# Load order, raw buffers, early counts and late gates in the second mixture of an attention and two-mixture kernel

## Chip, cores and metric

One core of a Trainium2 chip runs the whole program. The metric is device time in microseconds (us), the median of three runs.

## The reference

```
def _attn_ref(q, k, v):                 # 2 x 8 heads x 576 positions x 64
    scores = q @ k.T / 8, masked to the last 64 positions; softmax; @ v
def _moe_ref(x, domain_probs, w1, w2):  # 1152 rows x 512, 4 experts, F = 1024
    p = domain_probs / sum;  out = sum over e of p[:, e] * (relu(x @ w1[e]) @ w2[e])
def _moe2_ref(x, w_skip, w_gate, w1, w2):   # 8 experts
    do_compute = (x @ w_skip) > 0
    e_idx = argmax(x @ w_gate);  gate_w = softmax(x @ w_gate)[e_idx]
    out = x;  out[row] += gate_w * (relu(x[row] @ w1[e_idx]) @ w2[e_idx])   # where do_compute
```

In the first mixture every expert works on every row. In the second each row goes to one expert at most, so the kernel sorts rows by expert and works on blocks of 128 of them. With these inputs the eight experts get 116, 207, 129, 66, 298, 17, 114 and 51 rows.

## The kernel before, in words

The inputs are f32. Each operand is split into a high part of type f32r and a low part (the rest), and a product is three matmuls: high by high, high by low, low by high. ScalarE (ACT) writes the high part as a copy, VectorE (DVE) the low part as a subtraction. So a weight goes through a load by SP into a `raw` tile of 512 KB (`w_load`, L310), a copy by ACT (`hi`, L331, 1024 columns) and a subtraction by DVE (`lo`, L335); only then is the raw tile free. An expert has four chunks of first weights (L315 in the trace) and four of second weights (L317). Two sets of weight tiles, `wa` and `wb`, serve the experts in turn, and `w_pass` (L987) adds the loads and splits of one expert's first or second weights.

There are two rings of raw tiles: `raw`, four tiles in memory that is there from the start, and `raw2` (`M["raw"]`), four tiles in memory that `open_moe2` (L829) opens. `extra` in `w_pass` picks the ring. `open_moe2` closes the pool `h` (the 18 KB a partition of `x2`, and 12 KB each of `hh` and `hl`) and the pool `rt` with tiles of the routing, and opens in their place, from the right, `mg` (18 KB), `mo` (20 KB) and `mr` (16 KB, `raw2`). A tile in a pool that lies where a closed pool was waits for all instructions on the closed pool's tiles, also for those that the program lists later.

The order of work on every engine is written by a planner (`Plan`, L92). `add` hands it an operation with an engine, an assumed duration, what it reads and writes, a priority and a slack that is added to its ready time. `run` places the operations one by one, each time the one that can start first (priority breaks ties), and then emits them sorted by planned start. An engine executes its own operations in just that order. On ACT and DVE an operation of priority 0 or more may not run over the ready time of one of negative priority by more than 0.2 (L162). Loads count 1.46 on SP and 1.1 latency, apart from early ones (`early`, the first weights of expert 3 and later), which are put on an engine "X" that costs nothing else. Operations on X, such as `open_moe2` and `counts`, only fix a place in the program.

The first plan covers attention, the first mixture, the routing and block 0 of expert 0 of the second mixture. Each later expert has one plan for its first block (`block`, L881) and, if it has more rows, further ones under a branch: `tails` (L1084) asks whether it has more than 128. A block takes 20 matmuls of its first product, then transposes (`tr`, L927): ACT copies the product out (`hr`, L921), PE transposes it (L938), ACT and DVE write the high and low part of `ht` (L942, L945); this is done in two pieces. 24 matmuls of the second product follow, and DVE multiplies by the gates and adds (L979). Rows are fetched by indirect DMAs of GpSimd (POOL; `gather`, L845) and written by others (`scatter`, L854). During an expert's block its plan also holds the loads and splits of the next expert's weights and the transposes of the next rows (`xpose`, L861).

The routing (`route`, L625) runs once for each of nine row tiles t: logits, best expert, rank, and a product `tab` (L742) that puts row numbers (its columns 0 and 1) and gates (columns 2 to 4, the gate in three bf16 parts) into a table. For the last two tiles the gate columns are done late: `gate` (L723), `spread` with its `wx` (L737), `tab`. `idx` (L791) makes the row numbers, `num` (L803) the counts, `rest` (L812) the gates and the scatter's row numbers. `counts` (L1048) loads the packed counts into a register of every engine (L1050), and `hint` (L1077) tells PE's instruction fetch which way a later branch will go. After the last expert comes a deep section (L1121) under a branch of its own, for experts with more than 384 rows; here it is jumped over.

## Time and profile before

| | |
|---|---|
| median of three runs | 675.88 us (675.45 to 675.97) |
| the profiled execution | 672.51 us |
| its span, first to last instruction | 670.8 us |
| granted TensorE clock, mean | 0.984 |
| PE busy | 628.2 us, 94% |
| second mixture | from 486.9 us to the end |

Times in the rows are us from the span's start. PE is TensorE's matmuls, PEld its weight loads, SPq the queue of SP. A bracket at the end of a row gives how long the engine stood idle before it and what released it. [...]

### The profile page before, as it was taken

The numbers are of one execution on the slowest core, as the hardware profiler recorded it, in microseconds if no ns is written. First come the engines' busy times: TensorE is split into PE (matmuls) and PEld (weight loads), VectorE is DVE, ScalarE is ACT, GpSimd is POOL, SyncE is SP. The second block draws the span as 40 slices with busy tenths as digits, with TensorE's granted clock in tenths as the row PEclk, the third lists the DMA queues.
The fourth block names the chain that finished last, engine by engine and source line by source line (L and its number), as shares of the span: only waits on it lengthen the run. The fifth ranks groups of instructions, "written<-read, shape, count | busy, mean of one in ns | idle before, by whom it ended". The sixth has DMA issues, their size and how long they took to land. (4 is left out here: it accounts for less than half of the span.)

```text
span 670.8 us, 9656 instructions
## 1 busy us (share of the span) xinstructions
PE 628.2 (94%) x3652; PEld 552.8 (82%) x3652; DVE 323.8 (48%) x699; ACT 237.0 (35%) x492; POOL 91.5 (14%) x112
## 2 busy tenths in 40 slices
PE   6889999999999999999999999999987899899783
PEld 6788899898989898989898989898965678687573
DVE  5997932137312136212136336265576575654661
ACT  4974741035202033202033202124326465634550
POOL 6541320000000000000000000000043142312510
PEclk9999999999999999999999999999989999899987
DMA  9668000008300005200004210113339957961631
GB/s 219 159 164 241 23 4 1 0 1 270 106 1 1 0 1 176 75 1 1 0 1 165 87 64 33 48 47 104 129 131 308 360 185 227 303 252 39 209 112 29
DMA packets 55851, 71.69 MB, mean 107 GB/s; under 512 B 32953, under 2 KB 32953, under 8 KB 55776
## 3 DMA queue, kind: packets, MB, share of 16 engines
q1 hardware_dynamic: 52912, 62.17, 29.1%
q0 software_dynamic: 2864, 8.54, 4.4%
q8 instruction: 44, 0.72, 0.4%
q14 instruction: 31, 0.25, 0.1%
HBM read 64.00 MB, written 7.47 MB: 107 GB/s over the span
## 5 line engine op out<-in xcount | busy, mean ns | idle before, releaser
L523 PE MATMUL mm<-xth,wa1h 128*128 128x384 f32 (+1 forms) x416 | 137.4, 330 | 0.0
L523 PE MATMUL mm<-xtl,wa1h 128*128 128x384 f32 (+1 forms) x416 | 135.3, 325 | 0.0
L523 PE MATMUL mm<-xth,wa1l 128*128 128x384 f32 (+1 forms) x416 | 135.2, 325 | 0.0
L529 ACT ACTIVATE hh<-mm 128x384 fp32r<-128x384 f32 (+1 forms) x104 | 48.5, 466 | 234.5 <-PE mm L523 225.9
L544 PE MATMUL mm<-wa2h,hh 128*128 128x512 f32 (+1 forms) x296 | 116.9, 395 | 0.0
L544 PE MATMUL mm<-wa2h,hl 128*128 128x512 f32 (+1 forms) x296 | 115.0, 389 | 0.0
L544 PE MATMUL mm<-wa2l,hh 128*128 128x512 f32 (+1 forms) x296 | 114.9, 388 | 0.0
L531 DVE SCALAR_TENSOR_TENSOR hl<-mm,hh 128x384 fp32r<-128x384 f32 (+1 forms) x104 | 54.5, 526 | 121.7 <-ACT hh L529 121.6
L523 PEld LDWEIGHTS mm<-xth,wa1h 128*128 128x128 f32 x416 | 78.3, 188 | 0.7
L523 PEld LDWEIGHTS mm<-xtl,wa1h 128*128 128x128 f32 x416 | 78.2, 188 | 0.5
L523 PEld LDWEIGHTS mm<-xth,wa1l 128*128 128x128 f32 x416 | 78.2, 188 | 0.0
L544 PEld LDWEIGHTS mm<-wa2h,hl 128*128 128x128 f32 x296 | 55.7, 188 | 12.4
L544 PEld LDWEIGHTS mm<-wa2l,hh 128*128 128x128 f32 x296 | 55.8, 189 | 11.1
L544 PEld LDWEIGHTS mm<-wa2h,hh 128*128 128x128 f32 x296 | 55.8, 188 | 11.0
L556 DVE SCALAR_TENSOR_TENSOR x<-mm,prob,x 128x512 f32<-128x512 f32 (+1 forms) x28 | 20.5, 732 | 91.2 <-PE mm L544 91.2
L766 POOL DMA_INDIRECT x<-scr,id x1 | 1.2, 1242 | 360.3 <-DVE id L783 360.3
L331 ACT CAST wa2h<-raw 128x1024 fp32r<-128x1024 f32 x32 | 33.3, 1053 | 28.0 <-PE mm L544 18.6
L335 DVE TENSOR_TENSOR wa1l<-raw,wa1h 128x1024 fp32r<-128x1024 f32 x31 | 36.9, 1220 | 9.6 <-ACT wa1h L331 9.0
L335 DVE TENSOR_TENSOR wa2l<-raw,wa2h 128x1024 fp32r<-128x1024 f32 x30 | 36.2, 1219 | 7.0 <-ACT wa2h L331 6.8
L331 ACT CAST wa1h<-raw 128x1024 fp32r<-128x1024 f32 x30 | 30.3, 1047 | 22.5 <-DMA raw<-in_moe_w_dram 16.0
L855 POOL DMA_INDIRECT out_dram<-xg,ids x11 | 16.1, 1460 | 86.9 <-DVE xg L979 59.5
L444 POOL TENSOR_TENSOR s<-s,mx 128x512 f32<-128x512 f32 x18 | 20.2, 1122 | 50.1 <-DVE mx L441 23.0
(203 smaller groups left out, 917.8 us busy)
## 6 DMA issues: line engine op xcount, KB each, us to landing
raw<-in_moe_w_dram SPq DMA_DIRECT2D x96, 512.0 KB, 5.5
scr<-x SPq DMA_DIRECT2D x9, 256.0 KB, 2.1
out_dram<-x SPq DMA_DIRECT2D x9, 256.0 KB, 2.3
qn<-in_q_dram SPq DMA_DIRECT2D x8, 256.0 KB, 4.0
kn<-in_k_dram SPq DMA_DIRECT2D x8, 256.0 KB, 4.1
vn<-in_v_dram SPq DMA_DIRECT2D x8, 256.0 KB, 4.7
qn<-in_q_dram SPq DMA_DIRECT2D x2, 128.0 KB, 4.4
kn<-in_k_dram SPq DMA_DIRECT2D x2, 128.0 KB, 4.4
```

What stands on the lines that cost most here:

```text
L331: (POOL.tensor_copy if hpool else DVE.tensor_copy if hdve else ACT.copy)(out=aps()[0], in_=b.tile)
L335: (POOL if pool else DVE).tensor_tensor(out=l, in0=b.tile, in1=f32(h), op=ALU.subtract)
L444: add("POOL", 1.0, lambda: POOL.tensor_tensor(out=s.tile, in0=s.tile, in1=mx[:, 3].unsqueeze(2).to_broadcast([128, HP, 128]), op=ALU.mult) ...
L523: PE.matmul(out=ps[:, 0:n], lhsT=wa[a][:, kk, f * 128:(f + 1) * 128], rhs=x[:, kk, g0:g0 + n], start=(i == 0), stop=(i == 3 * KC - 1))
L529: add("ACT", c_act(n), lambda: ACT.activation(out=hh[:, f, 0:n], in_=ps[:, 0:n], func=ACTF.Relu), rd=[ps], wr=[("hh", f)], prio=-1)
L531: add("DVE", c_dve(n), lambda: DVE.scalar_tensor_tensor(out=hl[:, f, 0:n], in0=ps[:, 0:n], scalar=0.0, in1=f32(hh[:, f, 0:n]), op0=ALU.max ...
L544: PE.matmul(out=ps[:, 0:c1 - c0], lhsT=x[:, f, o:o + 128], rhs=wa[a][:, f, c0:c1], start=(f == 0 and i == 0), stop=(f == FC - 1 and i == 2))
L556: DVE.scalar_tensor_tensor(out=z, in0=y, scalar=prob[:, t, e:e + 1], in1=z, op0=ALU.mult, op1=ALU.add)
L766: add("POOL", 1.0, lambda: POOL.indirect_dma_start(out=R["x0"], out_offset=None, in_=scr[0:128 * (GT + 1), :], in_offset=bass.IndirectOffs ...
L855: add("POOL", 1.0, lambda: POOL.indirect_dma_start(out=out, out_offset=bass.IndirectOffsetOnAxis(ap=R["ids"][0:n, j, e:e + 1], axis=0), in ...
```

## The change

- Load order: an early load costs 0.0 instead of 0.01 in the planner.
- Raw buffers: second weights of every expert from 1 on go to `raw2` (before: from 2 on, by a counter).
- Gates: those of the last two tiles, and `rest`, are added inside block 0 of expert 0, and read the low part of the second piece of `ht` (`htl`, 4). The tiles they use move from the pool `rt` to `rc`, with a `wy` of their own beside `wx`. Masks move to an attention pool.
- Counts and hint: `counts` no longer waits for the second product of expert 0, and `hint` for expert 0 follows the second group of its first product. `num` writes a third value, loaded as `nv[2]`: the last expert has more than 128 rows, or one has more than 384.
- The transposes beside expert 0's second product come after its group 3.
- The last two transposes and logits of the routing get a negative slack.
- The deep section goes inside the last expert's branch, with a hint to PE and POOL; so does that expert's third gather.

```diff
--- before.py
+++ after.py
@@ -317,7 +317,7 @@
                 SP.dma_start(out=b.tile.rearrange("p (a n) -> p a n", a=2),
                              in_=src[c * 256:(c + 1) * 256, :].rearrange("(a p) n -> p a n", p=128))
 
-        add("X" if early else "SP", 0.01 if early else 1.46, f, rd=["M"] if extra else [], new=[b], prio=prio)
+        add("X" if early else "SP", 0.0 if early else 1.46, f, rd=["M"] if extra else [], new=[b], prio=prio)
         return b
 
     def w_split(b, ring, key, part, c, prio, pool=False, after=(), hpool=False, hdve=False):
@@ -593,8 +593,8 @@
                                ("ex", [128, E2], F32), ("tm", [128, E2], F32), ("gj", [128, TT + 1], F32),
                                ("oj", [128, TT], F32), ("r", [128, 128], BF16), ("g", [128, 4], F32),
                                ("gb", [128, 4], BF16), ("w", [128, 5, E2], BF16),
-                               ("wx", [128, TT, 5 * E2], BF16)):
-                R[nm, i] = rt_p.tile(sh, dt, name=f"{nm}{i}", tag=f"{nm}{i}", bufs=1)
+                               ("wx", [128, TT, 5 * E2], BF16), ("wy", [128, TT, 3 * E2], BF16)):
+                R[nm, i] = (rt_p if nm in ("x2t", "m8", "i8", "tm", "gj", "wx") else rc_p).tile(sh, dt, name=f"{nm}{i}", tag=f"{nm}{i}", bufs=1)
         R["rpr"].pool = rt_p
 
     def route_consts():
@@ -649,10 +649,10 @@
                               start=(kk == 0), stop=(kk == KC - 1), skip_group_check=True)
 
             w = k1 - k0
-            add("PE", 0.11 * w, tr, rd=[(key, t), "ident"], new=[p], prio=P, slack=sl)
+            add("PE", 0.11 * w, tr, rd=[(key, t), "ident"], new=[p], prio=P, slack=sl if k0 == 0 else -0.45)
             add("ACT", c_act(128 * w), cp, rd=[p, "R"], wr=[K("x2t")], prio=P)
             p.close()
-            add("PE", 0.19 * w, lg, rd=[K("x2t"), "wr"], wr=["lg"], prio=P, slack=sl)
+            add("PE", 0.19 * w, lg, rd=[K("x2t"), "wr"], wr=["lg"], prio=P, slack=sl if k0 == 0 else -0.25)
 
         def top():
             l, i8 = R["lg"], T("i8")
@@ -734,13 +734,14 @@
         def spread(c0, c1, pr, after=()):
 
             e0, n = c0 * E2, (c1 - c0) * E2
+            wx = lambda: T("wy" if c0 else "wx")[:, :, 0:n]
             add("DVE", c_dve(TT * n) + 0.01, lambda: DVE.tensor_tensor(
-                out=T("wx")[:, :, e0:e0 + n],
+                out=wx(),
                 in0=T("w")[:, c0:c1].rearrange("p c e -> p (c e)").unsqueeze(1).to_broadcast([128, TT, n]),
                 in1=T("oj").unsqueeze(2).to_broadcast([128, TT, n]), op=ALU.mult),
                 rd=[K("oj")] + [K("w0")] * (c0 == 0) + [K("w1")] * (c1 == 5), wr=[K(("wx", c0))], prio=pr)
             add("PE", max(0.11, TT * n / 2400), lambda: PE.matmul(
-                out=R["tab"].rearrange("p j c e -> p j (c e)")[:, :, e0:e0 + n], lhsT=T("r"), rhs=T("wx")[:, :, e0:e0 + n],
+                out=R["tab"].rearrange("p j c e -> p j (c e)")[:, :, e0:e0 + n], lhsT=T("r"), rhs=wx(),
                 start=(t == 0), stop=(t in (GT, TT - 1)), skip_group_check=True),
                 rd=[K("r"), K(("wx", c0)), *after], wr=[("tab", c) for c in range(c0, c1)], prio=pr, slack=sl)
 
@@ -755,7 +756,7 @@
                 spread(0, 5, 2)
             else:
                 spread(0, 2, 1)
-                later.append(lambda: (gates(["idg"], 15), spread(2, 5, 15, ["idg"])))
+                later.append(lambda: (gates(["idg", ("htl", 4)], 15), spread(2, 5, 15, ["idg"])))
 
         late.append(weigh)
         if t != TT - 2:
@@ -795,8 +796,6 @@
             DVE.tensor_scalar(out=R["idg"], in0=a, scalar1=0.0, scalar2=None, op0=ALU.max)
 
         add("DVE", 0.45, idx, rd=[("tab", 0), ("tab", 1)], wr=["idg"], prio=-1)
-        for f in later:
-            f()
         add("PE", 0.03, lambda: PE.matmul(out=R["pf"][:, 0:E2], lhsT=R["ones"], rhs=R[o], start=True, stop=True),
             rd=[o], wr=["pf"], prio=-4)
 
@@ -804,20 +803,25 @@
             n, x, sm = R["pf"][0:1, 0:E2], R["lvx"], R["lvs"]
             DVE.tensor_tensor(out=x, in0=n.unsqueeze(1).to_broadcast([1, 6, E2]), in1=R["lvt"], op=ALU.is_gt)
             DVE.tensor_reduce(out=sm[:, 1:2], in_=x[:, 5], axis=AX.X, op=ALU.max)
+            DVE.tensor_tensor(out=sm[:, 2:3], in0=sm[:, 1:2], in1=x[:, 1, E2 - 1:E2], op=ALU.max)
             DVE.scalar_tensor_tensor(out=x, in0=x, scalar=1.0, in1=R["lvw"].unsqueeze(1).to_broadcast([1, 6, E2]),
                                      op0=ALU.mult, op1=ALU.mult, accum_out=sm[:, 0:1])
-            DVE.tensor_copy(R["cnt"][0:1, E2:E2 + 2], sm)
+            DVE.tensor_copy(R["cnt"][0:1, E2:E2 + 3], sm)
             DVE.tensor_copy(R["cnt"][0:1, 0:E2], n)
 
+        add("DVE", 1.0, num, rd=["pf"], wr=["cnt"], prio=16)
+
+    def route_gates():
         def rest():
-            tb, a, b = R["tb"], R["a"], R["b"]
-            DVE.tensor_copy(tb[:, :, 2:5], R["tab"][:, :, 2:5])
-            DVE.tensor_tensor(out=b, in0=tb[:, :, 2], in1=tb[:, :, 3], op=ALU.add)
-            DVE.tensor_tensor(out=R["gates"], in0=b, in1=tb[:, :, 4], op=ALU.add)
+            a, b = R["a"], R["b"]
+            DVE.tensor_copy(b, R["tab"][:, :, 2])
+            DVE.tensor_tensor(out=b, in0=b, in1=R["tab"][:, :, 3], op=ALU.add)
+            DVE.tensor_tensor(out=R["gates"], in0=b, in1=R["tab"][:, :, 4], op=ALU.add)
             DVE.tensor_scalar(out=b, in0=a, scalar1=0.0, scalar2=4097.0, op0=ALU.is_lt, op1=ALU.mult)
             DVE.tensor_tensor(out=R["ids"], in0=a, in1=b, op=ALU.add)
 
-        add("DVE", 0.84, num, rd=["pf"], wr=["cnt"], prio=16)
+        for f in later:
+            f()
         add("DVE", 1.25, rest, rd=["idg"] + [("tab", c) for c in range(2, 5)], wr=["gates", "ids"], prio=20)
 
 
@@ -878,7 +882,8 @@
             p.close()
         return x
 
-    def block(e, j, xg, x, small=False):
+    def block(e, j, xg, x, small=False, amid=None):
+
 
         ring, key = rings[e], rkey[e % 2]
         mm_, ht = M["mmx"] if j else mm_r, M["ht"].buf()
@@ -945,7 +950,7 @@
             add("DVE", c_dve(w * n), lambda: DVE.scalar_tensor_tensor(
                 out=ht[:, s, n:2 * n], in0=p[:, 0:w, 0:n], scalar=0.0, in1=f32(ht[:, s, 0:n]), op0=ALU.max,
                 op1=ALU.subtract),
-                rd=[p, ht, (ht, "h", c0)], wr=[(ht, "l", c0)], prio=-1)
+                rd=[p, ht, (ht, "h", c0)], wr=[(ht, "l", c0), ("htl", c0)], prio=-1)
             p.close()
 
         hrs = [g1(*pieces[0])]
@@ -954,6 +959,8 @@
             if nxt:
                 hrs.append(g1(*nxt))
         x.close()
+        if amid:
+            amid()
         nh = 2 if e == E2 - 1 else 1
         halves = [(mm_.buf(), slice(h * DM // nh, (h + 1) * DM // nh)) for h in range(nh)]
         parts = [[] for _ in halves]
@@ -991,16 +998,11 @@
         src = ((w1, w2) if kd == "m" else (m1, m2))[p - 1][e]
         ring, key = (wa, "wa") if kd == "m" else (rings[e], rkey[e % 2])
         for c in range(4):
-            extra = False
-            if kd == "r" and e > 1:
-                extra = nw[0] % 8 > 3
-                nw[0] += 1
+            extra = kd == "r" and e > 0 and p == 2
             st = KN["w2s"] if (kd, e, p) == ("m", 0, 2) else 2.5
             b = w_load(src, p, c, prio + st * c, extra, early=kd == "r" and e > 2 and p == 1)
             w_split(b, ring, key, p, c, prio + st * c, pool=(kd, e, p) == ("m", 0, 2) and KN["w2pool"][c],
                     after=["idg"] if kd == "r" and e == 1 else [])
-
-    nw = [0]
 
     with tc.manual_schedule():
         w_pass("m", 0, 2, KN["w2p"])
@@ -1046,7 +1048,7 @@
         nv = []
 
         def counts():
-            for i, m in ((E2, 8 ** E2 - 1), (E2 + 1, 1)):
+            for i, m in ((E2, 8 ** E2 - 1), (E2 + 1, 1), (E2 + 2, 1)):
                 nv.append(nc.values_load(R["cnt"][0:1, i:i + 1], min_val=0, max_val=m,
                                          skip_runtime_bounds_check_because="levels of all experts, packed"))
 
@@ -1074,36 +1076,73 @@
                 scatter(e, j, x, 64)
                 plan.run()
 
+        def further(e):
+
+            return nv[2] > 0 if e == E2 - 1 else over(e, 2)
+
         def hint(e):
 
-            tc.mark_branch_hint_location(f"more{e}", hint=over(e, 2), engines=[PE.engine])
+            tc.mark_branch_hint_location(f"more{e}", hint=further(e), engines=[PE.engine, POOL.engine] if e == E2 - 1 else [PE.engine])
 
         def ahead(e):
-            add("PE", 0.05, lambda: hint(e), rd=[("g2", 0)], wr=[("g2", 1)], prio=10.0)
+            if e:
+                add("PE", 0.05, lambda: hint(e), rd=[("g2", 0)], wr=[("g2", 1)], prio=10.0)
+            else:
+                add("PE", 0.05, lambda: hint(e), rd=["nv", ("g10", 1)], wr=[("g10", 2)], prio=10.0)
+
+        def more(e, xt):
+            for j in (1, 2):
+                with tc.If(over(e, 4)) if j == 2 else ExitStack():
+                    if j == 2 and e == E2 - 1:
+                        xgs[e, j] = gather(e, j)
+                    if j == 2 or xt is None:
+                        xt = xpose(xgs[e, j], 0)
+                        plan.run()
+                    rows(e, j, xgs[e, j], xt)
 
         def tails(e, xt):
 
-            with tc.If(over(e, 2), label=f"more{e}", preferred_fallthrough_block=True):
-                for j in (1, 2):
-                    with tc.If(over(e, 4)) if j == 2 else ExitStack():
-                        if j == 2 or xt is None:
-                            xt = xpose(xgs[e, j], 0)
+            with tc.If(further(e), label=f"more{e}", preferred_fallthrough_block=True):
+                if e < E2 - 1:
+                    more(e, xt)
+                else:
+                    with tc.If(over(e, 2)):
+                        more(e, xt)
+                    with tc.If(nv[1] > 0):
+                        deep()
+
+        def deep():
+
+            for e in range(E2):
...
+                            scatter(e, j, x)
                             plan.run()
-                        rows(e, j, xgs[e, j], xt)
 
         for e in range(E2):
             last = e == E2 - 1
-            xgs[e, 2] = gather(e, 2, 7, [("g2", 0)] if not last else [])
+            if not last:
+                xgs[e, 2] = gather(e, 2, 7, [("g2", 0)])
             if last:
                 plan.run()
                 rows(e, 0, xgs[e, 0], xts[e, 0])
                 tails(e, None)
                 continue
-            block(e, 0, xgs[e, 0], xts[e, 0])
+            block(e, 0, xgs[e, 0], xts[e, 0], amid=None if e else route_gates)
             if e == 0:
-                add("X", 0.0, counts, rd=["cnt", ("g2", 0)])
+                add("X", 0.0, counts, rd=["cnt"], wr=["nv"], slack=1.5)
             ahead(e)
-            xts[e, 1] = xpose(xgs[e, 1], XP, [("g2", XE)])
+            xts[e, 1] = xpose(xgs[e, 1], XP, [("g2", XE if e else 3)])
             if e:
                 w_pass("r", e + 1, 1)
                 w_pass("r", e + 1, 2)
@@ -1111,29 +1150,13 @@
                 for j in range(2):
                     if e + d < E2:
                         xgs[e + d, j] = gather(e + d, j, 0 if e else 2 * d + j - 1 + (d == 1 and j), [("g10", 0)] if e else [])
-            xts[e + 1, 0] = xpose(xgs[e + 1, 0], XP, [("g2", XF)])
+            xts[e + 1, 0] = xpose(xgs[e + 1, 0], XP, [("g2", XF if e else 3)])
             scatter(e, 0, xgs[e, 0])
             plan.run(**(OFF if e else dict(SP=1.75, PE=1.4, ACT=2.1, POOL=0.6, DVE=0.6)))
             if e == 0:
                 route_ps.close()
                 M["mmx"].pool = ctx.enter_context(tc.tile_pool(name="ps_x", bufs=3, space=PSUM))
             tails(e, xts[e, 1])
-        with tc.If(nv[1] > 0):
...
 
 
 # ---- launch: one core; inputs and outputs as the reference has them ----
```

## Rows read from the trace of the kernel before

**Rows 1.** The page, part 1: busy time, share and count by engine
```profile
PE 628.2 (94%) x3652; PEld 552.8 (82%) x3652; DVE 323.8 (48%) x699; ACT 237.0 (35%) x492; POOL 91.5 (14%) x112
```

**Rows 2.** Busy time in stretches: experts 0, 1, 3, 4, 5, 6, then four others
```profile
core 0: us, PE busy (x) PEld busy (x) DVE busy (x) ACT busy (x) POOL busy (x), PEclk, DMA share, GB/s
486.90:507.55 20.65, 15.55 (x69) 11.83 (x69) 16.50 (x53) 5.85 (x9) 8.00 (x8) 0.92 0.54 166
507.55:536.75 29.20, 25.89 (x120) 20.38 (x120) 17.32 (x19) 16.04 (x21) 6.95 (x5) 1.00 0.98 343
560.73:574.20 13.47, 13.24 (x65) 10.69 (x65) 10.79 (x13) 10.62 (x15) 4.88 (x4) 1.00 0.56 127
574.20:591.65 17.45, 14.74 (x65) 12.11 (x66) 12.48 (x13) 11.11 (x14) 5.85 (x4) 0.90 0.83 286
615.24:628.53 13.29, 13.14 (x66) 10.58 (x64) 11.15 (x13) 8.81 (x13) 8.22 (x4) 1.00 0.28 70
628.53:650.03 21.50, 15.18 (x65) 12.12 (x65) 13.50 (x15) 11.11 (x14) 3.76 (x3) 0.84 0.62 212
496.20:499.50 3.30, 3.06 (x10) 2.57 (x10) 3.16 (x8) 0.09 (x1) 2.70 (x2) 0.50 0.56 173
581.50:584.90 3.40, 3.12 (x10) 2.64 (x11) 2.81 (x3) 2.02 (x4) 1.67 (x1) 0.50 1.05 406
636.20:642.90 6.70, 4.07 (x12) 3.38 (x13) 3.69 (x4) 4.28 (x6) 0.00 (x0) 0.50 0.81 297
618.00:626.00 8.00, 8.00 (x44) 6.63 (x43) 6.67 (x8) 6.68 (x10) 5.29 (x2) 1.00 0.27 79
```

**Rows 3.** Waits of PE, 486 to 661 us: total us, times, longest
```profile
PE pt L938 <- ACT hr L921: 10.4, 4, 5.4
PE mm L897 <- PEq L1086: 3.2, 2, 3.0
...
PE tab L742 <- DVE wx L737: 1.4, 1, 1.4
```

**Rows 4.** Timeline of ACT in expert 6: start, us, line, operation
```profile
634.54 1.04 ACT L331 CAST wa1h<-raw 128x1024 fp32r<-128x1024 f32 x1 [4.98 <-DMA raw<-in_moe_w_dram]
...
637.24 1.04 ACT L331 CAST wa1h<-raw 128x1024 fp32r<-128x1024 f32 x1 [1.66 <-DMA raw<-in_moe_w_dram]
638.19 0.59 ACT L921 ACTIVATE hr<-mm 128x512 f32<-128x512 f32 x1
```

**Rows 5.** Timeline of SP: loads of expert 7's first (L315) and second (L317) weights
```profile
618.13 0.34 SPq L315 DMA_DIRECT2D raw<-in_moe_w_dram  x1
626.08 0.37 SPq L317 DMA_DIRECT2D raw<-in_moe_w_dram  x1
626.50 1.62 SPq L315 DMA_DIRECT2D raw<-in_moe_w_dram  x3
```

**Rows 6.** Timeline of DVE: subtractions that free the four raw tiles
```profile
616.89 4.62 DVE L335 TENSOR_TENSOR wb1l<-raw,wb1h 128x1024 fp32r<-128x1024 f32 x4
```

**Rows 7.** The tile raw, 480 to 660 us: flight of its 52 loads
```profile
DMA to landing us min/median/max: 3.5/7.0/12.5
```

**Rows 8.** Timelines of PE and ACT in expert 0
```profile
490.86 0.24 PE L742 MATMUL tab<-wx,r 128*128 128x144 bf16 x1
...
490.13 0.60 ACT L921 ACTIVATE hr<-mm 128x512 f32<-128x512 f32 x1 [3.01 <-PE mm L897]
```

**Rows 9.** Line 1050: register loads on ACT, ns min/median/max
```profile
L1050 ACTq TENSOR_LOAD <-cnt x2: 291/380/468, 495.2 to 495.7; - x2
```

**Rows 10.** Busy time of DVE alone while it makes gates
```profile
491.78:496.40 4.62, 4.01 (x24) 0.97 0.31 86
```

**Rows 11.** Line 1121 on POOL; then a scatter's flight from the chain
```profile
L1121 POOLq EVENT_SEMAPHORE  x5: 17/43/43, 665.1 to 665.4; - x5
...
L1121 POOLq COMPARE_BRANCH  x1: 45/45/45, 662.3 to 662.3; - x1
L1121 POOLq INC_SWDGE_SEM  x1: 904/904/904, 665.5 to 665.5; - x1
...
650.21 3.43 DMA out_dram<-xg,ids
```

39 lines of the change are left out of this document (18 added, 21 removed).

## The prediction

> **What bounds the kernel now.** I read the head of the page first: TensorE (PE) is busy for 628.2 of 670.8 us [rows 1], so time can be won only where PE stands still or runs slowly. The table of stages [rows 2] shows where. While the second mixture runs (from 486.9 us on), the first block of expert 3 takes 13.47 us and that of expert 5 13.29 us; both are one full block with two transposes beside it, at full clock, and almost all PE work. I use their mean, 13.38, as the price of such a block. The same block takes 20.65 us for expert 0, 17.45 for expert 4 and 21.50 for expert 6. Expert 1 (two blocks) takes 29.20 us, of which PE works 25.89.
>
> The waits of PE say what ended this idle time [rows 3]: 10.4 us (longest 5.4) on `hr`, the copy that ScalarE (ACT) makes of a first product; 3.2 us on the branch of L1086; 1.4 us on the routing product `tab`. ACT is late with `hr` because of its in-order queue, as expert 6 shows [rows 4]: the splits of expert 7's first weights stand ahead of `hr`; two of them wait 4.98 and 1.66 us for their load, and `hr` starts the moment the third is through. The load is late because of SP's order [rows 5]: chunk 0 of the first weights goes out at 618.13, then SP waits until 626.08 for a buffer of the *second* weights, and chunks 1 to 3 leave only at 626.50. Their own buffers had been free since the four subtractions that run from 616.89 to 621.5 [rows 6]. [...]
>
> **The change part by part.** *Load order (L320).* In a plan that starts at 0, the four first-weight loads start at 0, 0.01, 0.02 and 0.03, and the first second-weight load at 0.00, so it is emitted second, as [rows 5] show. At cost 0.0 all four come first. SP then issues chunks 1 to 3 as the buffers come free, about 619 to 621.5 [rows 6], 5 to 7 us earlier, while the DMA engines are at a share of 0.27 [rows 2]. A load lands 3.5 us after issue at best and 7.0 at the median [rows 7], so the last is in by 628.5, when its split's turn comes. The second weights are issued no later than now, since their buffers come free after 621.5 anyway. I let expert 6 fall to the 13.38 us block plus 0.5 us for the branch into the last expert: 21.50 - 13.9 = -7.6. Expert 4 has the same order and falls to 13.38: 17.45 - 13.38 = -4.1. Experts 2, 3 and 5 have no such stop; 0. [...] Bounds: nothing won, and 0.5 more on expert 6.
>
> *Raw buffers (L994).* For e > 1 the new rule picks the same ring. New is that expert 1's second weights go into `raw2`, not into `raw`, and so no longer wait for expert 1's first splits. Two things follow in the planner. Its costs (1.46 for a load, 1.1 latency) make the first split ready 2.56 after `open_moe2`; it would end at 3.51; the first `hr` of expert 0 is ready at 3.38, and line 162 lets a low-priority operation start if it runs over by at most 0.2. So by 0.07 the split is put *ahead* of `hr` on ACT, and the second split and the value loads, by the same arithmetic, ahead of the first `ht`. The second thing is memory: x2, hh and hl give back 42 KB, but the pools opened there take 18 + 20 + 16 = 54 KB, so 12 KB of `raw2` lie where the pool `rt` was. The load must wait for the last reader of that pool, which after the change is the product `tab` at 490.86 [rows 8].
>
> Worked out: released at 491.1, landed at best 3.5 later [rows 7], 494.6; the split, 1.05 long as its neighbours in [rows 4], ends at 495.7; `hr`, 0.60 long, at 496.3. Today it ends at 490.73 [rows 8], so 5.6 us later. Then come the second split (497.4), three value loads of 0.29 to 0.47 us and their gaps (1.2; 498.6) [rows 9], `ht` (499.2), the second `hr` (499.8), PE's transposes (500.3). The first 12 of the 24 products of the second weights, 0.23 us each, run until 503.1.
>
> *Gates behind the first product.* In the stretch of [rows 10] VectorE (DVE) is busy 4.01 us: two `ht` subtractions of 0.69, the gates and their two `wx`, so 2.6 us for gates and `wx`, which delay PE by the 1.4 us of `tab` [rows 3]. Moved behind the second subtraction, the same work stands behind an `ht` that is itself late: third split, second `ht` and its subtraction (502.2), one weight subtraction of 1.2 that the planner fits in (503.4), gates and `wx` (506.0), `tab` at about 506.3. PE waits from 503.1 to 506.3 for it. Twelve products, two transposes and `tab` (4.1) follow, about 2 us longer at 1.2 GHz after these stops: 512.5, and 0.5 into expert 1: 513.0 instead of 507.55. Expert 0 thus costs **+5.4**. Bounds: -4.0 (the first rival) and +10.5 (the third).
>
> *Hint and counts early.* The 2.96 us in which PE waits for the branch of expert 0, most of the 3.2 us of [rows 3], go: the hint now stands some 12 us ahead of it. This is already in the 513.0. What is late next is `tab`. One more register load per engine and one more operation in `num` lie in waits; 0, at most +0.5. The slack of the last transposes is worth 0 to -0.5; taken as 0.
>
> *Expert 1.* Its second weights are there before it starts, and the 2 MB leave the stretch that has a DMA share of 0.98 [rows 2]. Its idle time, 29.20 - 25.89 = 3.3, falls to the two branches, 0.9: **-2.4**, between 0 and -2.9.
>
> *The end (L1121).* GpSimd (POOL) jumps over the deep section at 662.3 and is back at 665.1, then gives up its semaphores at 665.5 [rows 11]. With one branch, hinted, it arrives while the last scatter is in flight; that scatter bounds what is won: a larger one landed 3.43 us after its issue [rows 11], and the last goes out 0.9 before 662.3, so about 664.5 instead of 665.5: **-1.0**, between 0 and -2.8. The gather that leaves the last expert's common path is on no chain; 0. The masks' move is memory alone; 0.
>
> Sum: -4.1 - 7.6 + 5.4 - 2.4 - 1.0 = -9.7. The profiled run took 672.5 (span 670.8), so 662.8 by its clock; the median of three runs is 675.9, of which I take the same off: **666.2**.
>
> [...]
>
> **The rivals.** *First: ACT is not held in expert 0*, because the splits come behind `hr` and `ht` or the loads go out at `open_moe2`. PE would be through at about 501.8, but DVE has some 12.5 us from 491 on (gates and `wx` 2.6, four activation subtractions of 0.69, the index and gate tables some 2, four weight subtractions of 1.2), so expert 1 starts at about 503.5: -4.0. Sum -19.1: 656.8. For it: ACT is idle three quarters of expert 0 [rows 2], and 0.07 is a narrow margin. Against: that arithmetic, and the pool that must be released first.
>
> *Second, slower: the early loads don't help.* If the splits of experts 4 and 6 still wait, because the loads stay in flight until the block begins, both keep their time, and the stall of expert 0 remains: +5.4 - 2.4 - 1.0 = +2.0: 677.9. It decides from about 9 us of flight on (619.2 to 628.5); flights up to 12.5 us occur [rows 7]. Against: the DMA share of 0.27 just then.
>
> *Third: the loads of expert 0 go slowly.* Seven gathers run beside them. If the four take 7.0 us and more each [rows 7], every split ahead of an `hr` or `ht` is later by 3 to 4 us, some of it twice; I take +10.5 for expert 0: sum -4.6: 671.3.
>
> *Fourth: the change doesn't do what it says*; SP's order stays, and so do buffers and gates: 675.9.
>
> **How the numbers follow.** Forecast 0.52, its own range 662 to 670; first rival 0.28, third 0.10, second 0.07, fourth 0.03. Faster by over 0.2% (1.35 us, about what a measurement of this kernel can tell from no change): 0.90; within it 0.03; slower 0.07. The range of 656 to 671.5 takes in the forecast, the first and the third.
>
> **What would show each step.** Load order: SP's rows with four L315 in a row from 619 on; expert 4 and 6 at 13 to 14 us, clock 1.0. Raw buffers: the first L317 issued at about 491; ACT's `wa2h` ahead of the first `hr`, and PE idle for some 5 us before its transposes. Gates: `tab` with a wait of about 3 us in the second product. Hint: no PE wait on a branch after expert 0. End: POOL without a gap between its last branch and its semaphores. I am wrong if `hr` of expert 0 starts before 492, or if expert 6 still takes over 16 us.

## The result and the profile after

The changed kernel takes 662.5 us (median of 661.2, 661.5, 663.6 and 666.3); the kernel before took 675.7 beside it. The ratio on record is 0.985, with a 95% interval of 0.980 to 0.989 (the two medians alone give 0.981). The forecast was 666.2, in a range of 656 to 671.5: faster, as forecast, and by 3.7 us more than the central value.

The profiled execution is the slowest of the four: span 664.5 us against 670.8 before, so 6.3 us are there to be followed in the trace, and the rest of the 13.1 between the medians is not. First the stages (busy times in stretches; columns as in [rows 2]): experts 0 to 3, the first block of expert 4, its other rows, experts 5, 6 and 7, the end, and two stretches at half clock.

```profile
488.36:512.21 23.85, 17.17 (x68) 12.64 (x69) 14.56 (x52) 7.50 (x11) 8.24 (x7) 0.86 0.72 254
512.21:538.05 25.84, 25.40 (x120) 20.46 (x120) 18.92 (x21) 13.49 (x19) 7.27 (x5) 1.00 0.84 296
538.05:561.21 23.16, 22.71 (x120) 18.91 (x121) 14.34 (x18) 13.25 (x21) 6.36 (x5) 1.00 0.74 236
561.21:575.40 14.19, 13.26 (x65) 10.70 (x65) 11.56 (x14) 10.68 (x15) 4.87 (x4) 1.00 0.68 209
575.40:588.69 13.29, 13.22 (x64) 10.78 (x65) 11.66 (x12) 11.05 (x14) 5.12 (x4) 1.00 0.98 353
588.69:612.37 23.68, 22.16 (x117) 18.58 (x116) 6.75 (x10) 7.44 (x14) 2.74 (x2) 1.00 0.37 130
612.37:626.26 13.89, 13.14 (x65) 10.57 (x64) 11.68 (x14) 8.85 (x13) 6.14 (x2) 1.00 0.63 196
626.26:642.74 16.48, 13.38 (x65) 10.65 (x65) 14.69 (x16) 11.07 (x14) 7.06 (x5) 0.97 0.53 167
642.74:655.34 12.60, 12.60 (x72) 11.44 (x72) 1.99 (x6) 2.31 (x6) 0.00 (x0) 0.76 0.06 22
655.34:664.45 9.11, 0.00 (x1) 0.00 (x0) 1.05 (x3) 0.00 (x0) 0.92 (x1) 0.70 0.07 17
498.50:505.30 6.80, 6.11 (x19) 4.62 (x20) 3.54 (x4) 4.42 (x6) 4.63 (x4) 0.50 1.00 362
641.90:648.70 6.80, 5.96 (x20) 5.25 (x21) 1.04 (x1) 0.98 (x2) 0.79 (x1) 0.50 0.10 37
```

Four stages of the kernel before that [rows 2] leave out, by the same view: expert 2, the other rows of expert 4, expert 7, and the end.

```profile
536.75:560.73 23.98, 23.00 (x120) 18.83 (x121) 14.40 (x18) 13.33 (x21) 7.13 (x5) 1.00 0.68 238
591.49:615.24 23.75, 22.22 (x117) 18.57 (x116) 6.83 (x11) 7.48 (x14) 2.75 (x2) 1.00 0.45 173
650.03:659.93 9.90, 9.90 (x72) 9.13 (x72) 3.95 (x7) 2.31 (x6) 2.70 (x2) 1.00 0.16 55
659.93:670.78 10.85, 0.00 (x1) 0.00 (x0) 1.05 (x3) 0.00 (x0) 0.93 (x1) 0.66 0.08 18
```

What the reader is to see: expert 4's first block is now the plain block of 13.3 us, expert 1 has lost its waits, and expert 0 is longer. Expert 6 is shorter, but at 16.5 us not a plain block, and expert 7, whose work did not change, takes 2.7 us more because nearly half of it (642.74 to 648.7) runs at a granted clock of 0.50 (the column PEclk), against 1.00 in experts 1 to 5. The waits of PE (total us, times, longest) say the same:

```profile
PE pt L943 <- ACT hr L926: 5.5, 2, 4.8
PE mm L902 <- DVE wa2l L335: 2.9, 1, 2.9
PE mm L902 <- PEq L1105: 1.7, 2, 0.9
...
PE tab L743 <- DVE wy L738: 1.0, 1, 1.0
```

Of the 10.4 us on `hr` [rows 3] one stop of 4.8 is left, now in expert 0; the second row is the end of expert 6, to which the experiments come.

SP's timeline shows the load order at work: expert 7's four first-weight loads (L315) stand in a row, where [rows 5] had one, a gap of 8 us and three. Expert 1's second weights (the first row) wait for `raw2` until 492.70.

```profile
492.70 1.92 SPq L317 DMA_DIRECT2D raw<-in_moe_w_dram  x4
...
615.26 3.73 SPq L315 DMA_DIRECT2D raw<-in_moe_w_dram  x4
623.15 6.42 SPq L317 DMA_DIRECT2D raw<-in_moe_w_dram  x4
```

And ACT's timeline in expert 0 shows the split ahead of `hr`, with its wait on the load, then the second split, and a second `hr` (start, us, operation; idle time before it in brackets):

```profile
496.78 1.04 ACT L331 CAST wa2h<-raw 128x1024 fp32r<-128x1024 f32 x1 [8.19 <-DMA raw<-in_moe_w_dram]
497.73 0.59 ACT L926 ACTIVATE hr<-mm 128x512 f32<-128x512 f32 x1
498.22 1.03 ACT L331 CAST wa2h<-raw 128x1024 fp32r<-128x1024 f32 x1
499.74 0.60 ACT L947 ACTIVATE ht<-pt 128x512 fp32r<-128x512 f32 x1 [0.48 <-PE pt L943]
501.14 0.60 ACT L926 ACTIVATE hr<-mm 128x512 f32<-128x512 f32 x1 [0.81 <-PE mm L902]
```

### The profile page after: what moved, and what is told of

The parts are those of the page before. It is cut to its first block, busy times and chain, and to the rows that moved or that the text cites. A ratio compares the mean times of both kernels' runs of the same rounds, so it can differ in the third digit from the quotient of the medians.

```text
span 664.5 us, 9657 instructions
## 1 busy us (share of the span) xinstructions
PE 631.3 (95%) x3652; PEld 556.0 (84%) x3652; DVE 322.6 (49%) x700; ACT 235.9 (36%) x492; POOL 89.1 (13%) x111
## 5 line engine op out<-in xcount | busy, mean ns | idle before, releaser
L950 DVE SCALAR_TENSOR_TENSOR ht<-pt,ht 128x512 fp32r<-128x512 f32 (+2 forms) x27 | 15.1, 569 | 31.3 <-ACT ht L947 27.6
```

What stands on the lines that cost most here:

```text
L950: add("DVE", c_dve(w * n), lambda: DVE.scalar_tensor_tensor(out=ht[:, s, n:2 * n], in0=p[:, 0:w, 0:n], scalar=0.0, in1=f32(ht[:, s, 0:n]), ...
```

## The experiments

All ratios are against runs of the kernel before on the same chip (median 671.4 to 672.0 there). The runs were taken in three groups on three chips; the control stands in the first of them, so a difference to the control's median is one between chips for the other two groups. The stages of every profiled execution, in us, each from the first matmul of an expert to that of the next:

| kernel | ratio [95%] | e0 | e1 | e2 | e3 | e4 | e5 | e6 | e7 | end |
|---|---|---|---|---|---|---|---|---|---|---|
| before | 1 | 20.7 | 29.2 | 24.0 | 13.5 | 41.0 | 13.3 | 21.5 | 9.9 | 10.8 |
| after | 0.985 [0.980, 0.989] | 23.9 | 25.8 | 23.2 | 14.2 | 37.0 | 13.9 | 16.5 | 12.6 | 9.1 |
| after again | 0.986 [0.982, 0.989] | 25.0 | 25.9 | 23.1 | 14.1 | 37.1 | 13.8 | 16.8 | 11.4 | 9.2 |
| load order alone | 0.989 [0.986, 0.993] | 20.6 | 31.9 | 23.1 | 14.2 | 37.0 | 13.3 | 16.0 | 10.0 | 11.0 |
| raw2 undone | 0.989 [0.983, 0.994] | 21.3 | 29.9 | 23.1 | 14.1 | 37.1 | 13.3 | 16.2 | 11.4 | 9.2 |
| early hint undone | 0.991 [0.988, 0.993] | 26.2 | 25.9 | 23.2 | 14.3 | 36.9 | 14.5 | 15.0 | 11.5 | 9.1 |
| end undone | 0.991 [0.988, 0.994] | 23.7 | 25.9 | 23.2 | 14.4 | 36.8 | 13.5 | 17.8 | 12.5 | 11.6 |
| late gates undone | 0.986 [0.981, 0.992] | 22.1 | 26.7 | 23.1 | 15.1 | 38.3 | 13.7 | 17.2 | 11.4 | 9.1 |
| late loads for e7 | one run | 24.9 | 25.9 | 23.2 | 14.3 | 36.8 | 13.3 | 19.8 | 9.9 | 9.1 |
| hr first | 0.979 [0.976, 0.982] | 19.8 | 25.9 | 23.1 | 14.2 | 37.0 | 13.9 | 15.7 | 11.4 | 9.2 |
| hints early | 0.984 [0.981, 0.987] | 23.7 | 26.7 | 23.1 | 13.4 | 37.8 | 13.3 | 15.1 | 9.7 | 9.3 |
| hr first, hints early | 0.977 [0.974, 0.980] | 19.8 | 25.9 | 23.2 | 13.4 | 37.8 | 13.3 | 15.1 | 9.9 | 9.1 |
| the same, gates early | 0.976 [0.972, 0.979] | 18.9 | 25.9 | 23.1 | 13.4 | 37.9 | 13.3 | 15.1 | 9.9 | 9.1 |

**The changed kernel again.** 

> The changed kernel once more, as the control for the runs beside it. If the stages of its first trace are the kernel's own, expert 0 takes 23.9 us again, of which PE idles 4.8 before the first transposes, expert 6 takes 16.5 with 2.9 of idle time at its end, and the time is 661 to 666. If the half-clock stretch at 51.4 us of the first trace was of that execution alone, it is absent here and the second mixture starts about 1.1 us earlier.

Measured: median 663.0 (659.7 to 666.0). The stages repeat, except where the half clock falls: this time it stands at 497.5 to 500.9, 507.8 to 511.2 and 644.3 to 647.7, so expert 0 is 1.1 us longer and expert 7 1.2 shorter. The stretch at 50 us is here again; in five of the other traces of changed kernels it is absent, and the second mixture then starts 1 to 2 us earlier (486.4 to 486.9 against 487.6 to 488.6). So the stages are the kernel's own to about 1 us, and the place of the half clock is not.

**The load order alone**, in the kernel before.

```diff
-        add("X" if early else "SP", 0.01 if early else 1.46, f, ...
+        add("X" if early else "SP", 0.0 if early else 1.46, f, ...
```

> The kernel before with the load order alone (cost 0.0 instead of 0.01). Both theories: expert 4's first block falls from 17.3 to 13.3 us and the 5.4 us wait on hr in expert 6 goes. Theory A (the loads now fly beside PE's fetch of the code behind a branch and delay it): the branch into the next expert costs PE 0.7 to 0.9 us in experts 3 and 5 and 2 to 3 us at the end of expert 6, expert 7 runs partly at half clock, sum -5 to -6 us, about 670. Theory B (the deep section in the last branch makes the jump into expert 7 long): expert 6 ends with 0.9 us of idle time as before, sum -11 us, about 664.5.

Measured: 665.0, ratio 0.989. Expert 4 falls by 4.0 and expert 6 by 5.5: the order is the largest part of the gain. Against the kernel before beside it the time falls by 6.5 us, near theory A's 5 to 6 and not theory B's 11. Expert 6 still ends late: PE waits 1.75 us at the branch into expert 7 (0.9 before), with the deep section where it was. That is less than theory A's 2 to 3 us, and it is not a slower fetch: from the hint to the end of the second branch there it takes 7.0 us, against 7.3 before; the block is shorter and covers less of it. At the end of expert 3 PE waits 0.9 us at the branch, as theory A expected. Expert 5 loses nothing and expert 7 keeps its clock, against theory A; but from expert 5's hint to the end of its branch it takes 5.4 us instead of 3.6, and PE's queued matmuls cover it. Expert 1 is 2.7 us longer than before with the same instructions: its wait on `hr` came out at 2.3 us instead of 1.6, and it has two stretches of 3.4 us at half clock, one at its start (507.1 to 510.5) and one behind that wait (530.9 to 534.4), which the kernel before did not have in its trace.

**The end undone.**

```diff
+        with tc.If(nv[1] > 0):        # behind the last branch, as before
+            deep()
```

> The changed kernel with the deep section behind the last branch again, as before. My step: the end, from the last matmul to the end of the program, is 10.8 us again instead of 9.1, time +1 to +2. If the place of the deep section also makes PE's jump into expert 7 long (theory B), the idle time at the end of expert 6 falls from 2.9 to 0.9 us and expert 7 from 11.4 to 12.6 us to 9.9, and the sum is a gain of 2 to 3 us; if it is the loads beside the fetch and the late hint (theory A), the idle time stays at 1.8 to 3 us.

Measured: 667.2, ratio 0.991. The end takes 11.58 us instead of 9.11. The jump into expert 7 costs 3.5 us, not less, so theory B falls: the place of the deep section does not make it long. Of the difference in time the end's 2.4 us is this edit's; the rest shows in experts 6 and 7, that is in the late branch and the half clock behind it.

**Late loads for expert 7.** The old order for the four loads that fly during expert 5, all else as changed.

```diff
-        add("X" if early else "SP", 0.0 if early else 1.46, f, ...
+        add("X" if early else "SP", 0.01 * (early - 1) if early else 1.46, f, ...
...
-  early=kd == "r" and e > 2 and p == 1)
+  early=(kd == "r" and e > 2 and p == 1) * (1 + (e == 7)))
```

> The changed kernel with the old load order for expert 7's first weights alone (cost 0.01 for those four loads), so that three of the four no longer fly during expert 5. Theory A (loads in flight delay the fetch of the code behind a branch): from expert 5's hint to its branch it takes 3.5 us as in the kernel before instead of 6.2 to 6.3, and the idle time of 0.64 to 0.76 us at the end of expert 5 falls to 0.2; in exchange PE waits about 5 us for hr in expert 6 and the branch into expert 7 costs 0.9 us again, since there is time to fetch. Rival (the fetch is long for another reason, such as the place of the code): 6 us from hint to branch, 0.6 us or more of idle time.

Measured (one run, 665.2): PE's sequencer in expert 5. First the changed kernel, then this one (operation, count, its duration in ns, its start):

```profile
L1183 PEldq BRANCH_PREFETCH_HINT  x1: 40/40/40, 619.8 to 619.8; - x1
...
L1105 PEldq COMPARE_BRANCH  x1: 3987/3987/3987, 622.1 to 622.1; - x1
```

```profile
L1183 PEldq BRANCH_PREFETCH_HINT  x1: 40/40/40, 618.7 to 618.7; - x1
...
L1105 PEldq COMPARE_BRANCH  x1: 1507/1507/1507, 621.1 to 621.1; - x1
```

From the hint to the end of the branch it takes 6.3 us with the loads in flight (622.1 + 4.0 - 619.8), and 3.9 without. In the kernel before the hint is at 622.6 and the branch ends at 626.2: 3.6.

```profile
L1086 PEldq COMPARE_BRANCH  x1: 1173/1173/1173, 625.0 to 625.0; - x1
```

The DMA share over that time, from the hint to the end of the branch (the changed kernel, then this one, then the kernel before):

```profile
619.77:626.20 6.43, 5.74 (x30) 4.45 (x28) 4.89 (x6) 4.69 (x7) 1.04 (x1) 1.00 0.81 265
```

```profile
618.80:622.60 3.80, 3.80 (x23) 3.23 (x22) 2.47 (x4) 3.80 (x7) 1.69 (x1) 1.00 0.12 27
```

```profile
622.61:626.20 3.59, 3.59 (x23) 3.06 (x21) 2.48 (x3) 3.59 (x6) 1.14 (x2) 1.00 0.12 29
```

The trace also has the fetch itself: between hint and branch it shows one packet of 16 KB on a DMA queue that it calls `instruction`. In windows cut to that packet (the changed kernel, 623.70 to 624.60; this one, 619.88 to 621.12; queue, packets, MB, share of the 16 engines) it takes one engine's whole time:

```profile
q8 instruction: 1, 0.02, 6.1%
```

```profile
q8 instruction: 1, 0.02, 6.2%
```

The packet itself is not longer beside the loads (0.9 us against 1.2), and the branch ends 1.5 us behind it in both. It starts later: 3.9 us after the hint in the changed kernel, 1.1 in this one, 1.2 in the kernel before. In the eight traces that have the loads brought forward and the late hint, it starts 2.6 to 4.5 us after the hint, and the branch ends 5.0 to 6.9 after it, at DMA shares of 0.69 to 0.82.

Expert 5 is back at 13.3 us, expert 6 waits 3.7 us for `hr` again (19.8 us), and expert 7 runs at full clock (9.9); its branch leaves 1.45 us open, not the 0.9 that I expected. Theory A stands for expert 5: the loads, brought forward, hold up the start of the fetch of the code behind a branch, and PE pays for that. The order still wins 3 us in expert 6.

**Hints early.** The branch hints of experts 1 to 7 go behind the first third of the first product, 7 to 8 us earlier.

```diff
-  add("PE", 0.05, lambda: hint(e), rd=[("g2", 0)], wr=[("g2", 1)], prio=10.0)
+  add("PE", 0.05, lambda: hint(e), rd=[("g10", 1)], wr=[("g10", 2)], prio=10.0)
```

> The changed kernel with PE's branch hint of experts 1 to 7 some 35 instructions earlier, behind the first third of the first product instead of the second. If PE waits at the ends of experts 3, 5 and 6 because the fetch that the hint starts takes 4.8 to 6.4 us beside the loads, the idle time falls from 0.93, 0.76 and 2.85 us to 0.5 or less and 0.9, expert 7 keeps its clock, and the time is 4 to 6 us under the control. Rival: the fetch starts only when the branch is reached, or the early fetch is lost again; then the three waits stay as they are, within 0.3 us, and so does the time.

Measured: 661.1, ratio 0.984; the executions lie between 660.5 and 661.6, where those of the changed kernel spread from 659.7 to 666.3. The branch waits are gone, as these three stages show (experts 3, 6 and 7), and expert 7 keeps its clock:

```profile
561.20:574.59 13.39, 13.24 (x64) 10.70 (x65) 10.78 (x13) 10.78 (x15) 4.87 (x4) 1.00 0.67 206
...
625.62:640.72 15.10, 13.37 (x64) 10.64 (x65) 13.29 (x15) 11.16 (x14) 6.28 (x5) 1.00 0.57 195
640.72:650.37 9.65, 9.65 (x72) 9.08 (x72) 3.96 (x7) 2.30 (x6) 1.73 (x1) 1.00 0.09 29
```

The profiled span is 4.8 us shorter than the changed kernel's, the median only 1.9 under the control's; I expected 4 to 6. Part of the gain is given back to DVE: experts 1, 4 and 6 now have a stop of 0.85 to 0.86 us each that they did not have. In expert 4 the four weight subtractions and the `ht` behind them run at the same time as in the changed kernel (577.8 and 582.3); PE only arrives earlier and waits. DVE in this kernel (in the changed one these two start at 577.77 and 582.32), then PE's row:

```profile
577.76 4.63 DVE L335 TENSOR_TENSOR wa1l<-raw,wa1h 128x1024 fp32r<-128x1024 f32 x4 [0.26 <-PE mm L902]
582.30 0.69 DVE L950 SCALAR_TENSOR_TENSOR ht<-pt,ht 128x512 fp32r<-128x512 f32 x1
```

```profile
583.14 0.63 PE L943 MATMUL pt<-ident,hr 128*128 128x128 f32 x4 [0.86 <-DVE ht L950]
```

**hr first.** The splits of expert 1's second weights are planned behind expert 0's block; loads and buffers stay.

```diff
-        w_pass("r", 1, 2)                  # ahead of block(0)
+                w_pass("r", 1, 2)          # behind block(0)
...
-  hi, rd=[b], wr=[(key, part, "h", c)]
+  hi, rd=[b] + ([("htl", 4)] if after and part == 2 else []), wr=[(key, part, "h", c)]
```

> The changed kernel, with the splits of expert 1's second weights placed behind all four of ScalarE's operations of expert 0's block; loads and buffers stay. If the split that stands ahead of hr on ScalarE is what holds PE (my step), the 4.8 us before the first transposes fall under 0.7, expert 0 falls from 23.9 to 18 to 19.5 us, and the time is 5 us under the control. Rival: DVE's queue (weight subtractions, gates, index tables) ends last anyway; then expert 1 starts no more than 2 us earlier, and the wait turns up before expert 1's first or second product.

Measured: 657.9, ratio 0.979, 5.1 us under the control. The 4.8 us are gone and expert 0 takes 19.8 us, just above what I expected, for `tab` is the next late thing: PE waits 2.5 us for it.

```profile
PE tab L743 <- DVE w L730: 2.5, 1, 2.5
```

So the place of these splits in ACT's queue cost the changed kernel 4 to 5 us in expert 0. The edit moves all four; which of them costs how much was not tried one by one.

**raw2 undone.** Expert 1's second weights back in `raw`.

```diff
-            extra = kd == "r" and e > 0 and p == 2
+            extra = kd == "r" and e > 1 and p == 2
```

> The changed kernel with expert 1's second weights back in the ring raw (as before the change), all else kept. My step (raw2 and its splits cost expert 0 its time and give expert 1 some back): the 4.8 us before expert 0's first transposes go, expert 0 falls from 23.9 to 19.5 to 21 us, and expert 1 rises from 25.8 to 29 to 32 us with waits on hr again; the sum is between -2 and +3 us. Rival (the stall of expert 0 comes from the late gates and the DVE queue, not from the raw buffers): expert 0 stays at 23 us or more.

Measured: 664.5, ratio 0.989. The 4.8 us are gone. Expert 0 takes 21.3 us, a little over what I expected, with a wait of 2.6 us at `tab` and one of 2.9 at its end. Expert 1 takes 29.9, within it, but its wait is one of 2.0 us on `ht`, which stands on ACT behind a split that waits for its load, and not one on `hr`. Their stretches:

```profile
487.60:508.85 21.25, 14.37 (x68) 10.57 (x68) 14.43 (x51) 6.81 (x10) 7.23 (x7) 1.00 0.60 193
508.85:538.74 29.89, 27.35 (x120) 21.85 (x120) 19.25 (x22) 15.18 (x20) 7.49 (x5) 0.94 0.90 321
```

Together 51.1 us against 49.7 and 50.8 in the two traces of the changed kernel, and the intervals of the times overlap: as it stands, the buffer rule moves a stall from expert 1 to expert 0 and wins no more than 1.4 us. (With `hr` first the two take 45.6.)

**Early hint undone**, the counts and expert 0's hint as before.

```diff
+                add("X", 0.0, counts, rd=["cnt", ("g2", 0)])
+            add("PE", 0.05, lambda: hint(e), rd=[("g2", 0)], wr=[("g2", 1)], prio=10.0)   # expert 0 too
```

> The changed kernel with the counts' register loads and PE's hint of expert 0 where they stood before (behind the first part of the second product). My step (the early hint removes the branch wait of 3.0 us): expert 1 starts 1.5 to 3.5 us later, waiting for the branch of expert 0, time +2 to +3. Rival (the branch is hidden anyway behind the late hr and tab in the changed kernel): no branch wait over 0.5 us, time within 1 us of the changed kernel.

Measured: 665.9, ratio 0.991, 2.9 us over the control, with intervals that overlap slightly; the profiled spans are alike (664.5 us against 664.5 and 664.2). The trace speaks for the rival all the same: PE's sequencer stands at the branch for 2.5 us from 509.8 on, but the matmuls queued ahead of it last until 514.1, and PE does not idle there.

```profile
L1102 PEldq COMPARE_BRANCH  x1: 2507/2507/2507, 509.8 to 509.8; - x1
L1102 PEldq EVENT_SEMAPHORE  x1: 51/51/51, 514.1 to 514.1; - x1
```

Expert 0 is longer, 26.2 us, since its granted clock is 0.80 in this trace and 0.86 in the two of the changed kernel. So the branch wait of the kernel before has gone from the changed one, but once `hr` and `tab` are late, the early hint is not what keeps it away; why the time is longer is not settled.

**Late gates undone.** They are called in `route_end` again, ahead of the first product's end.

```diff
-  later.append(lambda: (gates(["idg", ("htl", 4)], 15), spread(2, 5, 15, ["idg"])))
+  later.append(lambda: (gates(["idg"], 15), spread(2, 5, 15, ["idg"])))
...
+        for f in later:
+            f()
```

> The changed kernel with gates, wx and the second tab products where they stood before, ahead of the first product's end. DVE has nothing to do in 3.5 of the 4.8 us in which PE waits for expert 0's hr, so if the stall comes from ScalarE alone, the early gates fit into it: the wait on tab of 1.0 to 2.3 us in the second product goes, no new one comes, expert 0 falls by 1 to 2.5 us, time -1 to -2. Rival (the early gates hold DVE and with it the index tables and gathers, as the 1.4 us wait on tab before the change): a wait of 1.4 us or more in the first product, expert 0 no shorter.

Measured: 663.4, ratio 0.986, no different from the control. In the trace the wait on `tab` is gone and expert 0 takes 22.1 us, 1.7 and 2.8 less than in the two traces of the changed kernel; experts 1, 3, 4 and 6 are longer by 0.4 to 1.3 us each in that same trace, with the branch waits in 3 and 6. That the gates cost expert 0 something is shown; that this would ever shorten the kernel is not.

**Both edits, and gates early besides.**

> The changed kernel with both: ScalarE's splits of expert 1's second weights behind expert 0's block, and PE's hints of experts 1 to 7 early. If the two gains are of different places, they add: 5.1 and 1.9 us under the control's median of 663.0, so 656; by the profiled stages 5.3 and 4.5, so as low as 653. If DVE, whose four weight subtractions now end last in experts 4 and 6, takes back what the hint wins, no more than 1 us under the kernel with the first edit alone (657.9).

> As the kernel with both edits, and the gates ahead of the first product's end as before the change. With hr in time, the late gates cost a wait of 2.5 us on tab in the second product; early they cost a wait of 1.4 us in the first product (as in the kernel before). My reading: expert 0 falls by 1 to 2 us against the kernel with both edits, time -1 to -2. Rival: the early gates delay DVE's ht subtraction and weight subtractions by their 2.6 us, and expert 1 starts no earlier; within 0.5 us.

Measured: 655.9 (ratio 0.977) and 656.5 (ratio 0.976). The first is 2 us under `hr` first alone by median and 2.9 by profiled span (653.9 against 656.8), with overlapping intervals; it lies between the two expectations, nearer to adding up. The second cannot be told from the first in time; its expert 0 is 0.9 us shorter in the trace. The intervals of both lie below those of the changed kernel, so both beat it, and the kernel before.

## Why the prediction was right, and where not

Terms of the sum beside the two traces of the changed kernel, as differences to [rows 2] and the rows of before above:

| term | forecast | first trace | second trace |
|---|---|---|---|
| expert 0 | +5.4 | +3.2 | +4.3 |
| expert 1 | -2.4 | -3.4 | -3.4 |
| expert 4 | -4.1 | -4.1 | -4.0 |
| expert 6 | -7.6 | -5.0 | -4.7 |
| end | -1.0 | -1.7 | -1.7 |
| experts 2, 3, 5, 7 | 0 | -0.8, +0.7, +0.6, +2.7 | -0.8, +0.6, +0.5, +1.5 |
| start of the second mixture | 0 | +1.5 | +1.1 |
| sum | -9.7 | -6.3 | -6.5 |

**Load order: right in its mechanism, and the step behind it failed.** The four loads go out in a row and experts 4 and 6 no longer wait for `hr`, as the forecast said; expert 4 is exact. But I had named "expert 6 still takes over 16 us" as what would prove me wrong, and it takes 16.5. The step that failed is the price of 0.5 us for "the branch into the last expert". PE works 13.4 us there and then stands 2.9 at two branches, one behind the other. The profile puts that wait down to `wa2l`, but the third of those subtractions ended at 641.8 and the fourth ends at 642.9, after PE has gone on; PE's own second branch ends at 642.6, 0.15 ahead of its first matmul. First the changed kernel, then the kernel before:

```profile
L1183 PEldq BRANCH_PREFETCH_HINT  x1: 30/30/30, 634.4 to 634.4; - x1
...
L1105 PEldq COMPARE_BRANCH  x1: 2878/2878/2878, 636.3 to 636.3; - x1
...
L1062 PEldq COMPARE_BRANCH  x1: 2397/2397/2397, 640.2 to 640.2; - x1
```

```profile
L1160 PEldq BRANCH_PREFETCH_HINT  x1: 35/35/35, 642.6 to 642.6; - x1
...
L1086 PEldq COMPARE_BRANCH  x1: 592/592/592, 645.8 to 645.8; - x1
...
L1060 PEldq COMPARE_BRANCH  x1: 350/350/350, 649.5 to 649.5; - x1
```

The second branch ends 3.4 us after the first in the one (639.2 and 642.6) and 3.5 in the other (646.4 and 649.9). From the hint that makes 3.8 + 3.5 = 7.3 us before, and 4.8 + 3.4 = 8.2 after. PE's last matmul of expert 6 ends 6.5 us after the hint in the kernel before (649.1), and 5.5 after it in the changed kernel (639.9). So even with 7.3 us the plain block leaves 1.8 open, about what the load order alone shows (1.75), and the later fetch adds the rest: the slow expert 6 had hidden two fetches. Then the granted clock stands at 0.50 for 6.8 us, 6.0 of them in expert 7. I had counted what a stop costs in clock (before: 0.50 from 636.2 to 642.9 [rows 2]) as gained in expert 6, and did not ask whether a new stop behind it would cost it again.

That loads hold up the hint's fetch is shown in expert 5. In expert 6 the trace shows the late fetch too, but with other transfers beside it: from the hint to the end of the first branch the DMA share is 0.23 in the changed kernel and 0.25 with the load order alone, where it takes 3.8 us as before. In the changed kernel the first packet of code (here in its window, 636.78 to 637.73) starts 2.4 us after the hint, against 1.2 in the kernel before and 1.0 with the load order alone.

```profile
q8 instruction: 1, 0.02, 6.1%
```

It starts as the last packet of POOL's indirect transfers (queue q0) ends, 0.01 us apart at most, and so it does in all four traces with a stop of 2.85 us or more (2.4 to 3.6 us after the hint). In the five with a stop of 1.45 to 2.0 us it starts 1.0 to 1.7 after the hint. So gathers and scatters are what it seems to wait for there, which no run tried; an early hint takes the stop down to the 0.9 us of before.

The same step was missing for experts 3 and 5, which I put at 0: +0.7 and +0.6 are branch waits too. I weighed what the loads would meet in expert 0, namely gathers, and not the fetch of code. The rows above give the price of such a fetch: 3.4 to 6.3 us from the hint, or from the branch ahead, to the end of the wait. In expert 0 of the kernel before it was 8.6 us (hint at 498.8, the packet from 504.8 to 506.0, end of the branch at 507.4): the 3.0 us of its branch wait go with a late fetch as well.

**Expert 0: the chain was right in the main, the clock was counted in the wrong place.** Measured from the start of the second mixture, the first L317 goes out after 4.3 us (forecast 4.2), the first `hr` ends after 10.0 (9.4), the second transposes start after 13.4 (13.4), `tab` after 19.5 (19.4). That the second transposes agree is in part chance: the second `hr` waited 0.8 us for PE's products at half clock (the row at 501.14 above), where the forecast had ACT's own queue as the limit. From `tab` to expert 1 it takes 4.4 us; I had 6.7, with 2 us there for a lower clock. No run shows that term, nor the frequency named with it: the traces give the granted clock alone, and in the first one it stands at 0.50 from 498.5 to 505.3, ahead of `tab`, where the twelve products take 4.3 instead of 2.8 us inside the time that PE would have waited for `tab` anyway: the wait is 1.0 us, not 3. In the second trace part of the half clock falls behind `tab`, and the term comes to +4.3. So the mis-sized term is the clock's, by 1 to 2 us. The wait that I called decisive, ACT's split ahead of `hr`, is shown by the row at 496.78 and by `hr` first; the planner's margin of 0.07 that puts it there was not tried by itself.

**My first rival**, that ACT is not held, gave 656.8 for the whole. `hr` first measures 657.9, but with 19.8 us in expert 0, not the 16.7 that I gave it: `tab` and the gates take the rest.

**The third rival** (loads slowed by gathers, +10.5) did not come about. The loads of that time fly 3.9 to 9.3 us. The first one, for which ACT waits, took 4.0, and the other three landed ahead of their split's turn. They are longer than the 3.5 us of the best load before, then, but not where it counted; how much of that is the gathers' doing no run separates. The kernel before had loads beside gathers too: the four that go out from 497.6 us on, with gathers issued until 501.2, flew 4.6 to 7.3 us.

```profile
DMA to landing us min/median/max: 3.9/5.7/9.3
```

**Expert 1** fell by 3.4 instead of 2.4: its idle time is 0.4 us, not the two branches' 0.9, for one of those two waits (0.5 us at 560.7) stood at the end of expert 2, and PE's own work in it is 0.5 us less. **The end** fell by 1.7, not 1.0; POOL does have a gap there, which I had excluded: its last scatter is issued at 656.7 and it goes on at 659.3 behind the jump over the section. **The early hint**: the branch wait of 3.0 us is gone, as forecast, but in the changed kernel it would be hidden without the hint too, behind the late `tab`; what the hint is worth with `hr` first was not tried. **Expert 2** lost 0.5 us of idle time that I had not seen in it.

So the sum over the first profiled execution was too hopeful by 3.4 us: experts 6 and 7, the branches of 3 and 5 and the late start make it worse by 8.1, and experts 0, 1, 2 and the end better by 4.7. That the median came out lower than forecast, not higher, is luck as far as the terms go, and comes from the spread: the profiled executions of the changed kernel are its slowest ones (666.3 of 661.2 to 666.3; 666.0 of 659.7 to 666.0), and that of the kernel before was below its median. The kernel before was slow in that group, too: its median of 675.7 became 671.4 to 672.0 in the three later ones, while the changed kernel came out at 662.5 and 663.0. Beside the control the difference is 8.4 us, less than the 9.7 of the forecast. The traces show half-clock stretches in different places in the two, at 1.1 to 2.7 us each, which fits that spread; the other executions have no trace, so which stretches they lack stays open.

## What to carry to other kernels

When transfers are brought forward, ask what else uses the DMA engines just then, and count the fetch of code behind a branch among it: in expert 5 the time from PE's hint to the end of its branch was 6.3 us with the loads in flight and 3.9 without, and the packet on the `instruction` queue between them started 3.9 us after the hint instead of 1.1. Look at both, and put the hint early enough: 7 to 8 us earlier, it took the wait at the end of expert 6 from 2.9 us to 0.9 here. Where an in-order queue serves both a chain that PE waits for and work for later, look at which of them a planner's tie or small margin puts first; putting the later work behind was worth 5 us here. And price the first wait that lies open behind a stop that you remove: in expert 6 the stop of 5.4 us went with its 6.7 us at a granted clock of 0.50, but one of 2.9 us behind it was followed by 6.8 us at 0.50.

## What was not expected of the hardware

From hint to the end of PE's branch: 3.6 and 3.9 us at a DMA share of 0.12, 6.3 at 0.81. The packet with the code took about 1 us in each; what differed is when it started, 1.1 to 1.2 or 3.9 us after the hint. A branch behind that one, without a hint of its own, ended 3.4 and 3.5 us after the first in the two kernels shown. With the hint early (at 625.9 with *hints early*) both branches at the end of expert 6 took 0.4 us each:

```profile
L1105 PEldq COMPARE_BRANCH  x1: 441/441/441, 636.3 to 636.3; - x1
...
L1062 PEldq COMPARE_BRANCH  x1: 422/422/422, 640.1 to 640.1; - x1
```

After the same stop the clock came out differently: in the changed kernel PE's granted clock was 0.50 for 6.8 us (from 0.8 us ahead of expert 7's first matmul) after 2.9 us of idle time, in its second trace for 3.4 us after 3.1. After 0.9 us it stayed at 1.00 in the four traces with that stop, and after 1.75 us in the one with the load order alone; with `raw2` undone 3.4 us at 0.50 followed a stop of 1.9.
